# Taking the four 64x64 corners of TensorE diagonally in two attention products

## The chip, the cores and the metric

One core of a Trainium2 chip runs the kernel. The metric is device time in microseconds (us) of one execution; smaller is better. The median before is 263.3 us; executions of one kernel agree within 0.3%, and a change counts as faster or slower from 2% on. Shorter differences inside the kernel are read from the traces, which resolve single matmuls.

## The reference, cut to what matters

Inputs: q, k, v of 8 batches x 8 heads x 576 positions x 64, and two weight matrices, 512x2048 and 2048x512.

```python
q_s = exp(q - max(q, -1));  q_s = q_s / sum(q_s, -1)      # softmax over the 64 features
k_s = exp(k - max(k, 2));   k_s = k_s / sum(k_s, 2)       # softmax over the positions
kv  = einsum('bhsd,bhse->bhde', k_s, v)                   # the k-v product
x   = einsum('bhsd,bhde->bhse', q_s, kv)                  # x's product; heads side by side: 4608 x 512
h   = x @ w_in
out = (h * sigmoid(h)) @ w_out
```

## The kernel before

The two attention products have 64 rows and 64 columns of weights, a quarter of TensorE's 128x128 array. The kernel puts four of them into the array's four corners. A corner is a row half (the partitions that the operands come from) and a column half (the PSUM partitions of the output). In the k-v product `r` is the row half and `s` the column half; in x's product it is the other way round. Every corner writes a place of its own: another bank, or another half of the partitions.

```python
def kv(b, cc):                                   # 9 x 4 matmuls; kv_both is kv(b, 0), kv(b, 1)
    for j in range(J):                           # J = 9 groups of 64 positions, summed in PSUM
        for r in range(2):
            for s in range(2):
                nc.tensor.matmul(
                    out=PS[s * 64:(s + 1) * 64, 6 + r, cc * 128:cc * 128 + E1],          # E1 = 65
                    lhsT=ek[r * 64:(r + 1) * 64, j, (2 * cc + s) * D:(2 * cc + s + 1) * D],
                    rhs=vaug[r * 64:(r + 1) * 64, j, 2 * cc + s, :],
                    start=(j == 0), stop=(j == J - 1),
                )

def xt_mm(b, cc, col, n, bank, dst):             # one piece of n columns: 4 matmuls
    for r in range(2):
        for s in range(2):
            h = slice(s * 64, (s + 1) * 64)
            nc.tensor.matmul(
                out=PS[r * 64:(r + 1) * 64, bank + s, dst:dst + n],
                lhsT=kvn[b % 3][h, cc, r, :],
                rhs=st[b]["qT"][h, col // P:(col + n) // P, cc, r * 64:(r + 1) * 64],
            )

def xt(t, cc, eng=nc.scalar):                    # 512 columns: one or two pieces, then the copy out
    got = pieces(t)
    for b, col, n, dst in got:
        xt_mm(b, cc, col, n, 6, dst)
    xt_evac(t, cc, 6, got[0][3], TCH, got[0][3], eng)
# ... the feed-forward part: full-array matmuls of 256 columns in groups of eight (lines 368 and 468)
# ... a schedule that strews kv_both and xt between those groups, for the batch after next
```

The softmax here doesn't subtract the row's maximum and nothing guards it: scores larger than these inputs give would overflow.

Of the kernel before, what the change touches and what calls it, by code (L numbers as in the profile page):

```python
# [17 lines left out]
def kernel(  # L18
# [165 lines left out]

    def kv(b, cc):
        for j in range(J):
            for r in range(2):
                for s in range(2):
                    nc.tensor.matmul(  # L189
                        out=PS[s * 64:(s + 1) * 64, 6 + r, cc * 128:cc * 128 + E1],  # L190
                        lhsT=ek[r * 64:(r + 1) * 64, j, (2 * cc + s) * D:(2 * cc + s + 1) * D],
                        rhs=vaug[r * 64:(r + 1) * 64, j, 2 * cc + s, :],
                        start=(j == 0),
                        stop=(j == J - 1),
                    )
# [13 lines left out]
    def kv_both(b):  # L209
        kv(b, 0)  # L210
        kv(b, 1)
        kvcopy(b)
# [9 lines left out]
        return got  # L222

    def xt_mm(b, cc, col, n, bank, dst):
        for r in range(2):
            for s in range(2):
                h = slice(s * 64, (s + 1) * 64)
                nc.tensor.matmul(  # L228
                    out=PS[r * 64:(r + 1) * 64, bank + s, dst:dst + n],
                    lhsT=kvn[b % 3][h, cc, r, :],  # L230
                    rhs=st[b]["qT"][h, col // P:(col + n) // P, cc, r * 64:(r + 1) * 64],
                )
# [5 lines left out]
    def xt(t, cc, eng=nc.scalar):  # L238
# [4 lines that stand above are left out]
# [340 lines left out]
    trcopy(0, 0, 0, 5, 0, nc.scalar)  # L583
    trcopy(0, 0, 5, J, 1)
    kv(0, 0)
    kvcopy(0, 0, 1)
    tr(0, 1, 0, 5, 2)
    tr(0, 1, 5, J, 3)
    exp_k(0, 1)
    xt_mm(0, 0, 0, 320, 4, 0)  # L590
    xt_mm(0, 0, 320, 256, 0, 0)
    heat(3, 6)
    vcast(0, 1, nc.scalar, 0, 1)
# [257 lines left out]
```

## Time and profile before

| | before |
|---|---|
| median time | 263.3 us |
| TensorE busy | 252.6 us, 97% of the profiled span of 261.6 us |
| share of the end's chain: k-v (L189), x (L228) | 1.7%, 2.1% |
| one block of 72 k-v matmuls: first to last start | 0.592 us |
| one block of 8 x matmuls, two pieces of 256 columns: first to last start | 0.144 us |

"First to last start" of a block is taken from the records of the single matmuls in the trace. It is a better length than busy time here, since the records of some 17 matmuls (0.19 us each) overlap at any time in it. The records do not name the corner of a matmul. The lines behind the table are in the prediction.

### The profile page before, as it was taken

To read this page: it belongs to the slowest core of one execution; us is meant where nothing else is said; L and a number is where in the kernel's file an instruction comes from. 1 tells how busy PE (TensorE), PEld (TensorE's weight loads), DVE (VectorE), ACT (ScalarE), POOL (GpSimd) and SP (SyncE) were. 2 spreads that over 40 slices of the span, in tenths; PEclk is the share of its full clock that TensorE was granted. 3 is DMA by queue.
4 is the path that set the end of the run, shared out by engine and by line. 5 is a ranking of instruction groups with operands and counts; after the bars stand their busy time and mean duration, and the time that the engine had idled before them with its cause. 6 is when DMAs were issued, how large, how long until landed. Compare 5 with 4: busy or idle time off the path is not lost.

```text
span 261.6 us, 6410 instructions
## 1 busy us (share of the span) xinstructions
PE 252.6 (97%) x2732; PEld 203.2 (78%) x2732; DVE 207.7 (79%) x268; ACT 187.6 (72%) x212; POOL 65.7 (25%) x62
## 2 busy tenths in 40 slices
PE   8799999999999999999999999999999999999992
PEld 3457655656887888888888888888888888888881
DVE  2867797888997999799979997999798548855832
ACT  5766887898994799579957995799573748484610
POOL 1743791651160306030603060306000000000003
PEclk9999999999999999999999999999999999999999
DMA  7999999689979486957794869640534003300624
GB/s 244 335 192 297 299 319 333 259 184 391 307 278 238 111 220 230 205 142 189 262 230 118 218 233 167 180 89 3 90 76 87 3 0 78 85 3 1 139 64 120
DMA packets 35452, 45.89 MB, mean 175 GB/s; under 512 B 16208, under 2 KB 19984, under 8 KB 35424
## 3 DMA queue, kind: packets, MB, share of 16 engines
q1 hardware_dynamic: 29568, 33.69, 47.4%
q0 software_dynamic: 5616, 11.60, 17.0%
q8 instruction: 21, 0.34, 0.5%
q10 hardware_dynamic: 240, 0.20, 0.2%
q14 instruction: 7, 0.06, 0.1%
HBM read 36.70 MB, written 9.44 MB: 176 GB/s over the span
## 4 chain that ended last, share of the span: by engine, by line
PE 79%; DVE 6%; DMA 5%; issue 4%; POOL 3%; ACT 1%; POOLq 0%; DVEq 0%; ACTq 0%
PE PS L468 34%; PE PS L368 33%; PE PS L405 5%; DMA qt<-in_q_dram 5%; PE PS L276 2%; PE PS L228 2%; PE PS L189 2%; DVE h L346 1%; POOL W L545 1%; DVE S L442 1%; DVE GT L442 1%; DVE zq L148 1%; POOL out_dram L730 1%; POOL h L126 0%; DVE h L91 0%
## 5 line engine op out<-in xcount | busy, mean ns | idle before, releaser
L346 DVE TENSOR_TENSOR h<-PS,h 128x1024 f32<-128x1024 f32 (+1 forms) x45 | 54.0, 1199 | 13.0 <-ACT h L89 6.8
L468 PEld LDWEIGHTS <-GT 128*128 128x128 f16 x512 | 49.6, 98 | 6.8 <-issue 1.0
L368 PEld LDWEIGHTS <-WS 128*128 128x128 f16 x480 | 46.8, 98 | 7.2 <-issue 1.1
L468 PE MATMUL PS<-W,GT 128*128 128x256 f16 x384 | 49.1, 273 | 0.0
L368 PE MATMUL PS<-XS,WS 128*128 128x256 f16 (+1 forms) x360 | 46.3, 272 | 0.5 <-DVE h L346 0.5
L352 ACT ACTIVATE GT<-h 128x1024 f16<-128x1024 f32 (+1 forms) x45 | 46.1, 1047 | 0.3 <-DVE h L346 0.3
L89 ACT COPY h<-PS 128x1024 f32<-128x1024 f32 (+1 forms) x35 | 35.1, 1004 | 13.6 <-PE PS L368 13.1
L157 POOL TENSOR_TENSOR eq<-eq,rzq 128x1152 bf16<-128x1152 bf16 x13 | 27.8, 2135 | 58.2 <-DVE rzq L152 56.5
L468 PEld LDWEIGHTS <-S 128*128 128x128 f16 x384 | 37.1, 98 | 5.5 <-issue 1.0
L368 PEld LDWEIGHTS <-W 128*128 128x128 f16 x360 | 34.7, 98 | 4.8 <-issue 0.5
L468 PE MATMUL PS<-T,S 128*128 128x256 f16 x256 | 32.7, 273 | 0.0
L368 PE MATMUL PS<-XT,W 128*128 128x256 f16 (+1 forms) x240 | 29.5, 272 | 0.1
L352 ACT ACTIVATE GT<-PS 128x1024 f16<-128x1024 f32 (+1 forms) x15 | 15.3, 1017 | 18.9 <-PE PS L368 18.9
L91 POOL CAST vaug<-vt 128x1152 bf16<-128x1152 f32 x12 | 14.9, 1242 | 43.7 <-DMA vt<-in_v_dram 34.9
L108 ACT ACTIVATE eq<-qt 128x1152 bf16<-128x1152 f32 (+1 forms) x18 | 19.1, 1059 | 2.7 <-DMA qt<-in_q_dram 2.7
L730 POOL DMA_DIRECT2D out_dram<-ow x5 | 2.7, 546 | 72.5 <-DVE ow L715 72.5
L113 ACT ACTIVATE ek<-kt 128x1152 bf16<-128x1152 f32 x16 | 18.4, 1154 | 1.4 <-DMA kt<-in_k_dram 1.4
L148 DVE TENSOR_REDUCE zq<-eq 128x18 f32<-128x1152 bf16 x12 | 16.1, 1344 | 3.8 <-ACT eq L108 3.8
L258 PE MATMUL PS<-XT,W 128*128 128x288 f16 x128 | 16.6, 286 | 0.5 <-DVE XT L91 0.2
L468 PE MATMUL PS<-W,S 128*128 128x256 f16 x128 | 16.5, 273 | 0.0
L488 DVE SCALAR_TENSOR_TENSOR ow<-PS,sc 128x512 f32<-128x512 f32 x7 | 4.8, 691 | 14.4 <-ACT sc L484 14.4
L258 PEld LDWEIGHTS <-W 128*128 128x128 f16 x128 | 12.3, 97 | 4.9 <-issue 1.6
(78 smaller groups left out, 346.3 us busy)
## 6 DMA issues: line engine op xcount, KB each, us to landing
out_dram<-ow SPq DMA_DIRECT2D x64, 128.0 KB, 2.4
qt<-in_q_dram SPq DMA_DIRECT2D x12, 576.0 KB, 4.6
kt<-in_k_dram SPq DMA_DIRECT2D x12, 576.0 KB, 5.4
vt<-in_v_dram SPq DMA_DIRECT2D x12, 576.0 KB, 5.4
qt<-in_q_dram POOLq DMA_DIRECT2D x4, 576.0 KB, 10.6
kt<-in_k_dram POOLq DMA_DIRECT2D x4, 576.0 KB, 13.3
vt<-in_v_dram POOLq DMA_DIRECT2D x4, 576.0 KB, 12.7
W<-in_moe_w_out_dram POOLq DMA_DIRECT2D x4, 512.0 KB, 14.9
```

The lines of the kernel that those rows point to most:

```text
L89: eng.copy(out=o, in_=i)
L91: eng.tensor_copy(o, i)
L108: nc.scalar.activation(out=half(st[b]["eq"], cc)[:, :, g0:g1], in_=jgd(b, "qt", cc)[:, :, g0:g1], func=ACT.Exp)
L113: nc.scalar.activation(out=half(ek, cc), in_=jgd(b, "kt", cc), func=ACT.Exp)
L148: nc.vector.reduce_sum(out=z, in_=e, axis=AX.X)
L157: eng.tensor_tensor(out=e, in0=e, in1=r[:, :, :, None].to_broadcast([128, J, 2, D]), op=ALU.mult)
L258: nc.tensor.matmul(out=PS[:, 2 * (fb % 3) + n, 0:S // 2], lhsT=W1[:, c, fb * 128:(fb + 1) * 128], rhs=XTS[0][:, c, n * (S // 2):(n + 1) * ...
L346: nc.vector.tensor_tensor(out=four(t, i), in0=group_bank(t, True), in1=four(t, i), op=ALU.add)
L352: nc.scalar.activation(out=group_out(t, f, n), in_=x, func=ACT.Silu, scale=1.0 / XS)
L368: nc.tensor.matmul(out=PS[:, bank + p // 2, (p % 2) * HT:(p % 2) * HT + width(t)], lhsT=a[:, c, p * 128:(p + 1) * 128], rhs=bb[:, c, 0:wid ...
L405: nc.tensor.matmul(out=PS[:, 2 + tb, :], lhsT=GTS[t % 2][:, fc, tb * 128:(tb + 1) * 128], rhs=W2[:, fc, :], start=(fc == 0), stop=(fc == N ...
L468: nc.tensor.matmul(out=PS[:, bank, m * HN:(m + 1) * HN], lhsT=a[:, fc, m * 128:(m + 1) * 128], rhs=bb[:, fc, :], start=(first and fc == 0) ...
```

## The change

Its likely intent: neighbours in the program should not share a row half, so that a load of weights is never held up by a matmul that runs in the same rows. In each four, r = s comes first, then r != s. Only in the k-v product does the change follow it: its neighbours shared a row half before and no longer do. In x's product rows alternated before, and now the two middle matmuls of a four share one. Nothing else changes; line numbers after it move by one or two.

```diff
     def kv(b, cc):
         for j in range(J):
-            for r in range(2):
-                for s in range(2):
+            for i in range(2):
+                for r in range(2):
+                    s = r ^ i
                     nc.tensor.matmul(
...
     def xt_mm(b, cc, col, n, bank, dst):
-        for r in range(2):
-            for s in range(2):
+        for i in range(2):
+            for r in range(2):
+                s = r ^ i
                 h = slice(s * 64, (s + 1) * 64)
```

## The prediction

> **What bounds the kernel now.** I read the page first, then the chain of work that ended last, then the waits of TensorE, then the timeline of TensorE around the products that the change touches (line 189 is the k-v product, line 228 is x's product).
>
> The page, busy time by engine and the shares of the chain:
>
> ```profile
> PE 252.6 (97%) x2732; PEld 203.2 (78%) x2732; DVE 207.7 (79%) x268; ACT 187.6 (72%) x212; POOL 65.7 (25%) x62
> ...
> PE 79%; DVE 6%; DMA 5%; issue 4%; POOL 3%; ACT 1%; POOLq 0%; DVEq 0%; ACTq 0%
> PE PS L468 34%; PE PS L368 33%; PE PS L405 5%; DMA qt<-in_q_dram 5%; PE PS L276 2%; PE PS L228 2%; PE PS L189 2%; DVE h L346 1%; POOL W L545 1%; DVE S L442 1%; DVE GT L442 1%; DVE zq L148 1%; POOL out_dram L730 1%; POOL h L126 0%; DVE h L91 0%
> ```
>
> TensorE carries the end: 79% of the chain. Of that, the big feed-forward products (L468, L368) have two thirds of the span and the two changed lines some 2% each. The chain's own view prints them as 1.7% (L189) and 2.1% (L228) of 261.6 us, so 4.4 + 5.5 = 9.9 us. That is everything the change can reach, and most of it is arithmetic that stays.
>
> Waits of TensorE: every entry for a changed line. L228 does not appear at all.
>
> ```profile
> PE PS L189 <- ACT vaug L89: 0.3, 1, 0.3
> ```
>
> So these products are nearly never starved by another engine; what they cost is TensorE's own time. One steady stage of the chain (start, length, engine, line, count):
>
> ```profile
> 101.76 0.87 PE PS L368 x8
> 102.63 0.73 PE PS L189 x72
> 103.37 0.98 PE PS L368 x8
> ...
> 108.72 0.87 PE PS L368 x8
> 109.59 0.34 PE PS L228 x8
> 109.93 1.09 PE PS L468 x9
> ```
>
> A block of 72 k-v matmuls takes 0.73 us on the chain, and the group after it 0.98 instead of 0.87, so 0.84 us in all. A block of 8 x products takes 0.34, and the nine matmuls after it 1.09 where nine at 0.87/8 = 0.109 would take 0.98: 0.45 in all.
>
> Now the inside of the two blocks, from TensorE's timeline. The first answer below has a window that ends at 102.61, the second one at 102.64, the third covers the whole block; the fourth to sixth are an x block, cut at 109.64, at 109.70, and whole:
>
> ```profile
> 102.56 0.23 PE L189 MATMUL PS<-vaug,ek 64*64 64x65 bf16 x4
> ...
> 102.56 0.26 PE L189 MATMUL PS<-vaug,ek 64*64 64x65 bf16 x8
> ...
> 102.56 0.81 PE L189 MATMUL PS<-vaug,ek 64*64 64x65 bf16 x72
> ...
> 109.52 0.30 PE L228 MATMUL PS<-qT,kvn 64*64 64x256 bf16 x4
> ...
> 109.52 0.41 PE L228 MATMUL PS<-qT,kvn 64*64 64x256 bf16 x8
> ```
>
> Seventy-two matmuls of about 0.19 us each (the line's median is 193 ns) lie within 0.81 us, so some 17 are in flight at a time. They start in fours: four before 102.61, then four more. **All four corners already run together.** The x block says it too: four matmuls of 293 ns end 0.30 us after the first began, so their starts lie within 10 ns; the next four end 0.11 us later, and 0.11 us is what one stream of 256 columns takes in the full-array products (0.87/8 = 0.109). Four matmuls in a row would have taken 0.43.
>
> **What the Trainium skill says.** (1) "TensorE: Matmul & The Clock Gate", Part 3, The mechanism: matmuls in different tiles of the array run at the same time with starts about 4 ns apart, they start in program order, and a weight load overlaps matmuls in flight only when its row group differs. The first half agrees: the single records of the block at 102.56 show starts at 102.563, .567, .570 and .573. The second half is the obvious motive for the change, and the trace does not bear it out: k-v's order now is (row, column) (0,0), (0,1), (1,0), (1,1), so the second load has the row group of the matmul before it, yet its record starts at 102.565, 2 ns after that matmul, and is as long (103 ns) as the third, whose row group is new. (2) "TensorEngine Tiling (Array Packing)", Key Properties: changing the tiling mode drains TensorE. It agrees: the last full matmul before the block starts at 102.361, the first small one at 102.563, 0.20 us against the usual 0.109. The number of such switches does not change. (3) The first page again, "Wait — 56ns, not 53.3ns?": starts never come closer than about 25 ns however short the matmul. Not so here: 72 starts in 0.59 us are 8.3 ns apart.
>
> **The change, part by part.** It removes no instruction, adds none and moves no other engine's work: the same 576 k-v and 128 x pairs of weight load and matmul, permuted within each four. k-v goes to (0,0), (1,1), (0,1), (1,0): neighbours never share a row. x's product goes from (0,0), (1,0), (0,1), (1,1) to (0,0), (1,1), (1,0), (0,1): neighbours in a diagonal share nothing, but the middle pair now shares a row, where before rows alternated. Each output element has its own bank and partitions, and its sum over j keeps its order.
>
> *k-v.* The floor of the array: a full matmul of 256 columns takes 0.109 us, so 65 columns take about 0.0277 (estimate), and 18 fours take 0.50 us. Measured from first to last start: 0.592 us (102.563 to 103.155 in the records; the same 592 ns in six of the seven 72-blocks, 585 in the last). So at most 0.1 us a block could be won by any order. But the records say that the feed of instructions takes most of it: in the second half of the block the loads start evenly, 103.017, .025, .033, .042, .050, .058, .067: one pair of load and matmul every 8.33 ns. 71 x 8.33 = 591 ns, just the length of the block. In the first half the fours come every 32 ns on average (gaps of 36 and 29 by turns), hardly faster than 4 x 8.33 = 33.3. So the array waits for instructions by the middle of each block, and an order that lets it take a four in 29 instead of 32 ns only makes it catch up with the feed sooner. I allow 0 to 0.03 us a block: with 7 whole blocks and two halves in the prologue, 0 to 0.24 us.
>
> *x.* In the first four, the records show 134 ns to the second four: about 27 for the first weight load, which nothing can hide after the drain, and 107 for the stream. The second four's loads begin 27 ns into the block, under the first stream, and cost nothing. There is nothing in it to win: 0. If the shared row in the middle pair delayed that load, it would be by one load, 27 ns, in each of 16 first blocks: 0.4 us lost. I think it costs 0, since k-v has that very neighbourhood now and shows no delay.
>
> *Before and after.* Drains (0.09 us into the block, as much out of it) stay. The vector engine's wait for the last matmul moves by the few ns by which the last corner moves.
>
> Sum: between -0.24 and +0.4 us, most likely -0.05. Predicted 263.2 us.
>
> **Rivals.** *(A) The row-group rule holds and the loads are the bound.* Then k-v speeds up to the floor of 0.50 us: 0.09 x 8 = 0.7 us, 262.5 us. For it: an alternation of 36 and 29 ns that something in the array must cause. Against it: the even 8.33 ns of the second half. *(B) The diagonal pairs don't run four at once,* say because two column halves fed from different rows need something the straight pairs share. Then a k-v four takes two streams, 18 x 0.055 = 1.0 us in place of 0.59, +0.4 x 8 = 3.2 us, and each 512 columns of x take another 0.21 us, x 16 = 3.4 us: 270 us, +2.5%. Against it: all four are in flight at once already, (0,0) with (1,1) among them, so diagonals can share the array; only the order of issue is new. *(C) The reordering moves a wait.* Which matmul of a block carries the wait for a bank, and which ends it, changes; the block after may start some ns sooner or later, and the vector engine with it. TensorE waits 0.3 us for these lines in all, so at most +/-0.3 us.
>
> **Range and chances.** The three runs of the kernel before lie between 263.2 and 263.8, and that spread is larger than all effects I can derive. So the range is 262.7 to 263.8. Within 2% means 258.0 to 268.5. Faster than that would need over half of the 9.9 us on the path to vanish, below the array's floor: 1%. Slower needs rival B at full size: 2%. The rest, 97%, is "same".
>
> **What would show it.** In the changed profile: the 72-blocks of k-v still 0.81 us long, first to last start near 0.59 (0.50 would prove rival A, 1.0 rival B); x blocks still 0.41 long, with the second four 0.11 after the first; chain shares near 1.7% and 2.1%; same instruction count, 6410. The prediction is wrong if k-v's blocks get longer or shorter by over 0.05 us, or if a wait of TensorE by these lines appears that is not there now.

## The result, and the profile after

| | before | after |
|---|---|---|
| median of 4 runs each | 263.32 us (263.2 to 263.8) | 263.38 us (263.28 to 263.65) |
| ratio | | 1.000, 95% interval 0.998 to 1.002 |

The result is right, and the time is the same. (A ratio here is the mean time of one kernel's fast runs over that of the other's fast runs of the same rounds, so not quite the ratio of the medians quoted.)

The page of the changed kernel: busy times and the chain by line. The k-v product is now L190, x's product L230.

```profile
PE 251.8 (96%) x2732; PEld 203.1 (78%) x2732; DVE 208.0 (80%) x268; ACT 187.5 (72%) x212; POOL 65.6 (25%) x62
...
PE PS L470 34%; PE PS L370 33%; PE PS L407 5%; DMA vt<-in_v_dram 4%; PE PS L260 3%; PE PS L278 2%; PE PS L230 2%; PE PS L190 2%; DVE h L348 1%; DVE S L444 1%; DVE GT L444 1%; DVE zq L148 1%; SPq L97 1%; POOL out_dram L732 1%; ACT sg L252 1%
```

The chain still runs through the big products, and the two changed lines have their 2% each. The same stage of the chain as in the prediction (start, length, engine, line, count):

```profile
102.51 0.73 PE PS L190 x72
103.24 0.98 PE PS L370 x8
...
109.46 0.34 PE PS L230 x8
109.80 1.85 PE PS L470 x16
```

0.73 and 0.34 us, and 0.98 for the group after the k-v block: to the last digit the numbers of before. TensorE's timeline of the same blocks, with windows that end after the first four matmuls, after eight, and after all of them; then the first four and all eight of x:

```profile
102.44 0.22 PE L190 MATMUL PS<-vaug,ek 64*64 64x65 bf16 x4
...
102.44 0.26 PE L190 MATMUL PS<-vaug,ek 64*64 64x65 bf16 x8
...
102.44 0.81 PE L190 MATMUL PS<-vaug,ek 64*64 64x65 bf16 x72
...
109.39 0.30 PE L230 MATMUL PS<-qT,kvn 64*64 64x256 bf16 x4
...
109.39 0.41 PE L230 MATMUL PS<-qT,kvn 64*64 64x256 bf16 x8
```

Four at once, then four more, and the same 0.81 and 0.41 us. In the single records the first eight starts of this k-v block are at 0, 3 (before: 4), 7, 10, 53, 56, 59, 63 ns in both kernels, the fours after these follow each other every 29 to 39 ns in both, and a whole block measures 592 or 593 ns (585 and 586 in the last one).

One wait differs: TensorE's waits of the changed kernel have

```profile
PE PS L175 <- DVE eq L157: 1.5, 1, 1.5
...
PE PS L190 <- ACT vaug L89: 0.5, 2, 0.4
```

0.5 us in two waits where it was 0.3 in one, and 1.5 us for a transpose where it was 1.0. The longer wait for the transpose can't come from the change: TensorE's timeline shows that it ends before the first k-v matmul of the program has started. Before, then after:

```profile
8.65 0.68 PE L175 MATMUL PS<-ident,eq 128*128 128x128 bf16 x9 [0.96 <-DVE eq L157]
...
11.16 0.48 PE L189 MATMUL PS<-vaug,ek 64*64 64x65 bf16 x36 [0.33 <-ACT vaug L89]
```

```profile
8.67 0.68 PE L175 MATMUL PS<-ident,eq 128*128 128x128 bf16 x9 [1.52 <-DVE eq L157]
...
11.24 0.48 PE L190 MATMUL PS<-vaug,ek 64*64 64x65 bf16 x36 [0.39 <-ACT vaug L89]
```

The waits of the k-v product lie in the first 15 us too, where work hangs on the arrival of the inputs; x_runs2 below, with k-v's order of before, has two of 0.6 us together. A yardstick free of that is the distance from one k-v block to one three stages later, in the same trace. TensorE's timeline has, before,

```profile
102.56 0.81 PE L189 MATMUL PS<-vaug,ek 64*64 64x65 bf16 x72
...
181.14 0.78 PE L189 MATMUL PS<-vaug,ek 64*64 64x65 bf16 x72
```

and after

```profile
102.44 0.81 PE L190 MATMUL PS<-vaug,ek 64*64 64x65 bf16 x72
...
181.01 0.78 PE L190 MATMUL PS<-vaug,ek 64*64 64x65 bf16 x72
```

To the nanosecond the records give 78.575 us in both (102.563 to 181.138, 102.436 to 181.011). I call it the **three-stage distance** below; three k-v and six x blocks and all work between lie in it. So the change does nothing that these records show in the main loop. The question left is why the order is free: because any order is, or because this one is as good?

### The profile page after: what moved, and what is told of

Its sections match the earlier page's. It is cut to its first block, busy times and chain, and to the rows that moved or that the text cites. A ratio compares the mean times of both kernels' runs of the same rounds, so it can differ in the third digit from the quotient of the medians.

```text
span 261.5 us, 6410 instructions
## 1 busy us (share of the span) xinstructions
PE 251.8 (96%) x2732; PEld 203.1 (78%) x2732; DVE 208.0 (80%) x268; ACT 187.5 (72%) x212; POOL 65.6 (25%) x62
## 4 chain that ended last, share of the span: by engine, by line
PE 82%; DVE 7%; DMA 4%; ACT 2%; POOL 2%; issue 1%; SPq 1%; POOLq 0%; DVEq 0%; ACTq 0%
PE PS L470 34%; PE PS L370 33%; PE PS L407 5%; DMA vt<-in_v_dram 4%; PE PS L260 3%; PE PS L278 2%; PE PS L230 2%; PE PS L190 2%; DVE h L348 1%; DVE S L444 1%; DVE GT L444 1%; DVE zq L148 1%; SPq L97 1%; POOL out_dram L732 1%; ACT sg L252 1%
```

## The experiments

All start from the kernel before and alter only the order or the width of the changed products. Where one look was taken (no rounds), times are beside one run of the kernel before in the same call, the state of both is unknown (their granted clocks are 0.995 to 1.000), and they carry some tenths of a us of scatter (the kernel before alone: 263.12 to 263.76), so the block lengths and the three-stage distance decide.

### Each half of the change alone

`kv_only` has the diagonal order in the k-v product alone, `x_only` in x's product alone (the first and the second half of the diff above).

> The kernel before with k-v's order alone changed to the diagonal one, x's as before. Does the unchanged time hide two effects that cancel? Theory: no, blocks of 0.59 us, ratio 1.000 within the noise of +/-0.002. Rival G (k-v gains from alternating rows what x loses by the shared row in its middle pair): ratio 0.998 or less here and 1.002 or more in x_only.

> The kernel before with x's order alone changed. Theory: x blocks of two pieces of 256 columns stay at 0.144 us from first to last start, ratio 1.000 within +/-0.002. Rival G: ratio 1.002 or more, blocks 0.02 to 0.03 us longer.

Measured, five rounds: kv_only 263.12 us, ratio 0.9996 (0.9983 to 1.0010); x_only 263.24, ratio 1.0001 (0.9988 to 1.0013), before 263.21. Three-stage distances 78.574 and 78.576 us. The blocks of two pieces of 256 columns in x_only have 143 ns from first to last start, before 144. Nothing cancels; each half alone does nothing. Rival G is out.

### Two corners at a time, in the three possible pairs

Here the theory of the prediction (the feed of instructions limits a block, so the order is hidden) can be put to a harder test: with only two corners taking turns, the feed has time to spare, and a fault of the pair would show.

```diff
 kv_rows2:  for r in range(2):  for j in range(J):  for s in range(2):                 # a shared row half
 kv_cols2:  for s in range(2):  for j in range(J):  for r in range(2):                 # a shared column half
 kv_diag2:  for i in range(2):  for j in range(J):  for r in range(2):  s = r ^ i      # nothing shared
```

> From the kernel before: k-v's loop over r outermost, then j, then s, so that only two corners take turns, and the two share a row group: (0,0),(0,1),(0,0),(0,1)..., then the other row. Result stays right. Here the feed of 8.33 ns a pair of load and matmul (16.7 ns a step of two) is no longer the limit, the array is. Theory (order inside a step is free, corners only have to differ): a step of two takes 29 to 32 ns as a step of four does now, so 36 steps take 1.07 to 1.15 us from first to last start of a 72-block in place of 0.59, and the time is about 0.5 x 8 = 4 us longer, 267 us; the same as kv_cols2 and kv_diag2 within 0.03 us a block. Rival A (a load overlaps matmuls in flight only where its row group differs): every load waits for a stream of its row, a step takes about 54 ns, a block 1.95 us, 274 us, and kv_cols2 and kv_diag2 are far shorter.

> As kv_rows2, with s outermost: the two corners that take turns share a column half (one PSUM half, two banks) and differ in row group. Right result. Theory: 1.07 to 1.15 us a block, the same as kv_rows2, 267 us. Rival A: clearly shorter than kv_rows2, by up to 0.8 us a block.

> As kv_rows2, with the diagonal outermost: for i, for j, for r, s = r xor i, so the two corners that take turns share neither row nor column. Right result. Theory: 1.07 to 1.15 us a block, equal to the two others within 0.03, 267 us. Rival A: as kv_cols2, shorter than kv_rows2. If diagonal corners are the ones that can work together best (the motive of the change at its strongest), this one is the shortest of the three.

Measured: 265.09, 265.01 and 264.71 us beside 263.76; all right. TensorE's timeline of kv_rows2, then of kv_diag2:

```profile
103.27 1.04 PE L189 MATMUL PS<-vaug,ek 64*64 64x65 bf16 x72
```

```profile
102.86 1.04 PE L190 MATMUL PS<-vaug,ek 64*64 64x65 bf16 x72
```

The same length. From first to last start these blocks have 850, 849 and 851 ns, the three-stage distances are 79.288, 79.288 and 79.285 us. So a pair that shares a row half is neither slower nor faster than a diagonal one: rival A, that a load can't overlap a matmul of its own rows, is false here. (The 0.3 us by which kv_diag2's single time is shorter arise outside the three stages.)

But my number was wrong: I expected 1.07 to 1.15 us, 36 steps of 29 to 32 ns one after another, and a block took 0.85. The starts show how. A pair of one of these orders starts every 30 ns or so, but about 190 ns into a phase of 18 matmuls, when only 12 have started, two more starts follow after 6 to 9 ns, and for some 90 ns fours go by as in the full order. The next phase seems to have begun before the last one was done; kv_tags below tests that.

### One corner at a time, and with a tag on each

```diff
 kv_corner:  for r in range(2):  for s in range(2):  for j in range(J):
 kv_tags: the same, and
+                    n = E1 if j == 0 else E1 - 8 * r - 4 * s
-   out=PS[..., cc * 128:cc * 128 + E1]   rhs=vaug[..., :]
+   out=PS[..., cc * 128:cc * 128 + n]    rhs=vaug[..., 0:n]
```

> From the kernel before: k-v corner by corner, r and s outermost, j innermost, so that 9 matmuls in a row use one corner. Right result. It measures what the taking of turns is worth and whether a load can hide under a stream of its own corner. Theory: the loads hide (as they do in the full-array products), 72 steps of 29 to 32 ns, 2.1 to 2.3 us a block, +1.6 x 8 = 13 us, 276 us. Rival A: loads can't hide in their own row, 72 steps of 54 ns, 3.9 us a block, +26 us, 290 us.

> kv_corner again, but for j over 0 the four corners stream 65, 61, 57 and 53 columns (wrong result on purpose), so that the record of each matmul tells its corner. kv_rows2 and kv_corner came out shorter (0.85 and 1.58 us a block) than 36 and 72 steps one after another. Theory E (each corner has a short queue of its own, of about two pairs; the program is dealt out in order, but a corner starts its matmuls without regard to those of other corners that stand before them): matmuls of 61 columns start before the last two or three of 65 have, a few in each change of corner, block 1.55 to 1.6 us. Rival F (matmuls start strictly in program order; the shorter blocks come from faster steps in one corner): all of one width start before the first of the next.

kv_corner: 269.81 us beside 263.76, right. A block has 1.58 us from first to last start, less than both numbers expected. Its timeline:

```profile
105.06 1.77 PE L189 MATMUL PS<-vaug,ek 64*64 64x65 bf16 x72
```

In the main loop the time follows the blocks: 0.99 us longer each, three-stage distance 81.479 against 78.575, so +0.97 a stage. (The whole kernel is only 6.05 us longer in these single times, not 8 x 0.99 = 7.9: of the four blocks' worth, 4.0 us, before the main loop, 2.5 us show in the start of its first k-v block.)

kv_tags has blocks of 1.58 us again (269.47 us). Its output is wrong, which doesn't matter for the time. Now every record but those of the first j has its corner in its width: 9 matmuls of the first corner, all of 65 columns, come first in the program; then the second corner's first of 65 and eight of 61. Groups by shape in a window from the block's start (104.70) to 104.945; it holds all of the block's matmuls that had started by then:

```profile
L190 PE MATMUL PS<-vaug,ek 64*64 64x65 bf16 x8 | 0.4, 197 | 0.0
L369 PE MATMUL PS<-XT,W 128*128 128x256 f16 x1 | 0.3, 272 | 0.0
L190 PE MATMUL PS<-vaug,ek 64*64 64x61 bf16 x1 | 0.2, 193 | 0.0
```

A 61 has started when only eight 65s have, though ten 65s stand before it in the program. The starts from the records, in ns from the block's first: 65 at 0, 52, 88, 117, 150, 179, 185, 215; **61 at 237**; 65 at 244; 61 at 271; 65 at 276. So matmuls of different corners overtake each other. Theory E is borne out and rival F is not: at 237 two of the first corner's still wait (taking each corner by itself in program order). (The 65 at 185, 6 ns after another one where a corner takes some 30, must be the second corner's first; then three were waiting. None goes ahead of more in this block.)

### How far the overtaking reaches

If each corner has its own short queue, then the order of the program is free as long as no corner has more in a row than its queue holds. `kv_runs3` gives each corner three j in a row; `x_runs2` gives each corner both pieces of x in a row.

```diff
 kv_runs3:
-        for j in range(J):
+        for j0 in range(0, J, 3):
             for r in range(2):
                 for s in range(2):
+                    for j in range(j0, j0 + 3):
 x_runs2 (in xt):
-        for b, col, n, dst in got:
-            xt_mm(b, cc, col, n, 6, dst)
+        for r in range(2):
+            for s in range(2):
+                for b, col, n, dst in got:
+                    one matmul as in xt_mm
```

> k-v in runs of three: j in three groups of 3, and in each group corner by corner, three j in a row. Right result. Theory E: two waiting pairs of a corner don't stop the next corner, so a run of 3 (one at work, two waiting) costs nearly nothing: a 72-block of 0.60 to 0.65 us, time 263.3 to 264. Rival F: the third matmul of a run starts 62 ns after its first and those of the next corner after that, so 24 runs of about 62 ns and more, a block of 1.4 to 1.5 us, time 270.

> x's product from the main loop corner by corner: each corner takes both its pieces in a row (a run of two; the prologue's calls stay as they are). Right result. Theory E: a second piece waits in its corner's own queue while the next corner starts: a block of two pieces of 256 columns stays at about 0.15 us from first to last start and 0.41 in all, time 263.3. Rival F: the next corner's first piece can't start before this corner's second, 134 ns for the first corner and 107 for each other, about 0.45 us from first to last start, +0.3 us in each of 12 blocks of two pieces, 267 us.

kv_runs3: 263.89 us beside 263.35, right. Its timeline, and that of x_runs2's x block of two pieces:

```profile
102.69 0.90 PE L190 MATMUL PS<-vaug,ek 64*64 64x65 bf16 x72
```

```profile
109.74 0.42 PE L239 MATMUL PS<-qT,kvn 64*64 64x256 bf16 x8
```

First to last start is 0.708 us in kv_runs3 (0.682 in the last block): more than the 0.60 to 0.65 that I gave theory E, and half of the 1.4 to 1.5 of rival F. A run of three isn't quite free; it costs 0.095 us a stage (three-stage distance 78.860). The first four starts are at 0, 10, 20 and 30 ns. They must be the beginnings of the four corners, three places of the program apart, so the fourth corner begins 30 ns after the first instead of 10; and near the middle of the block two steps of four starts take 48 and 62 ns. x_runs2: 263.73 us beside 263.35, the block 0.154 us from first to last start in place of 0.144, where rival F asked for 0.45. The 10 ns are the later begin of the fourth corner (starts at 109.740, .746, .753, .760). Three-stage distance 78.640, +0.022 a stage for two x blocks. So a run of two costs next to nothing, and the permutation within a four, which gives no corner two in a row, nothing.

### What does limit a block

Two limits were candidates: the array (stream and load of weights) and the feed of instructions. `kv_short` streams half as many columns; `kv_wide` and `kv_wide_diag` stream 128, so that the array is the limit beyond doubt, in the straight and in the diagonal order.

```diff
 kv_short:      n = 65 if j == 0 else 33;  out=PS[..., cc * 128:cc * 128 + n],  rhs=vaug[..., 0:n]
 kv_wide:       out=PS[..., cc * 128:cc * 128 + 128],  rhs = the first 128 of the 130 columns of heads 2cc, 2cc + 1
 kv_wide_diag:  as kv_wide, with the changed kernel's loops
```

> From the kernel before, its order kept: for j over 0 the k-v matmuls stream 33 of the 65 columns (wrong result on purpose: the columns from 33 on keep the first j's sum). Same number of instructions. Theory (the feed of one pair of load and matmul every 8.33 ns is the limit): a 72-block stays at 0.59 us from first to last start, with loads evenly 8.3 ns apart sooner than before, time 263.3. Rival C (the stream in the array is the limit): a four takes half as long, a block 0.30 to 0.35 us, time 2 us shorter. Rival D (the loading of 64 weight columns, about 27 ns, is the limit of a corner): a block 0.50 to 0.52 us.

> From the kernel before, its order kept: every k-v matmul streams 128 columns (those of both heads of its pair) in place of 65 (wrong result on purpose for s = 1). Now the array and not the feed is the limit while all four corners are at work. Theory: a four takes 128 columns at 0.109 us per 256 = 55 ns, a block 17 x 55 + 27 + 10 = 0.97 us from first to last start; time +0.38 x 8 = 3 us, 266.3 us; kv_wide_diag is the same within 0.03 us a block. Rival A: the loads that share a row come late, a block is 1.2 us or more.

> As kv_wide with k-v's order of the changed kernel (diagonal fours). Theory: 0.97 us a block as kv_wide, within 0.03; so the change does nothing where the array is the limit either. Rival A, and the motive of the change: shorter than kv_wide by 0.1 us a block or more, and the time by 1 us or more.

All three are wrong on purpose. kv_short took 263.22 us beside 263.12; its timeline:

```profile
102.41 0.79 PE L190 MATMUL PS<-vaug,ek 64*64 64x65 bf16 x72
```

(0.79 and not 0.81, since the last record itself is shorter.) A block has 591 or 592 ns from first to last start as before (584 in the last), with half the stream. So the stream is not the limit, and this run's rival C is out. In its first half the fours come evenly every 31 to 32 ns (before: about 29 and 36 by turns), though streaming 33 columns takes only 14 ns (half of the 0.0277 us estimated for 65): something in a corner other than the stream takes 31 to 32 ns a matmul. That part of rival D holds; the weight load is its likely cause, but no run separates it from a fixed minimum of a corner.

In the second half the loads come one every 8.3 ns (at 405, 413, 421, 430, 438, 446 ns), as before; I had expected this even pace to begin sooner, and it doesn't. The stream doesn't set it, then. That it is the feed of instructions is my inference; no run changes the feed. And it doesn't set a block's length by itself, as the prediction's 71 x 8.33 = 591 ns has it. In the kernel before, the 68th load starts at 530 ns, 28 ahead of that sum's line (67 x 8.33 = 558), and then, in every 72-block but the last, there is a gap of 34 ns before the last four loads, whose cause the records don't show. The last block has no such gap; its last load starts at 563 ns and its last matmul still at 585. There the corners set the end. So two limits lie 5% apart, the 32 ns that a corner takes for its matmul in each four and the 33.3 ns of four loads at the even pace, and these runs don't say more exactly how they share a block.

kv_wide and kv_wide_diag took 265.64 and 265.24 us. TensorE's timeline of the one, then of the other:

```profile
103.19 1.20 PE L189 MATMUL PS<-vaug,ek 64*64 64x128 bf16 x72
```

```profile
102.80 1.20 PE L190 MATMUL PS<-vaug,ek 64*64 64x128 bf16 x72
```

989 ns from first to last start in both (0.97 expected), and a three-stage distance of 79.770 us in both. Fours come every 56 ns, the stream of 128 columns. Where the array is the limit and the feed has time to spare, the diagonal order is still worth nothing, as with two corners above. The feed, then, is not what hides the order. What fits all runs is that the corners work independently: a load waits for its own corner, whatever its neighbour in the program does, as far as the short queues reach.

## Why the prediction was right

The time (263.2 predicted, 263.38 measured) and the class were right. By its steps:

- **All four corners already run together; the x block has nothing to win.** Shown: 0.30 and 0.41 us in both kernels, and x_only alone is at ratio 1.0001. The fear of 27 ns for the shared row in x's middle pair was empty, as I thought.
- **A load may overlap a matmul of its own row half.** Right, and now shown where nothing could hide it: kv_rows2 and kv_diag2 have the same blocks.
- **The feed takes what an order could win, 0 to 0.03 us a block.** The number was right (0 to 1 ns in every whole block), but in part by luck. The even 8.33 ns is there, yet 71 x 8.33 meets the block's length to the nanosecond only because of the gap before its last four loads. I also supposed that another order might let the array take a four in 29 instead of 32 ns, and that the feed would then hide it. There is nothing to hide: the first fours are the same, and with the feed out of the way, in kv_rows2 and kv_diag2 and in both wide runs, the orders are still equal.
- **What I missed** is the overtaking. I thought of starts in program order, and so took the trace's neighbours for the program's, which the records can't tell. That is why I expected 1.07 us and more for two corners at a time and got 0.85. As kv_tags and kv_runs3 have it, permuting a four changes only the order in which four independent queues are handed one pair each.
- **Rival B** (diagonal pairs can't run at once, 270 us) was false; the prediction's **rival C** (a wait moves) did not show: the wait that grew most, by 0.5 us, ends before the first changed matmul, and the k-v product's 0.2 us more have their like in x_runs2, with the old order.

## What to carry to other kernels

Where the trace shows the corners of the array already starting together, expect little from permuting matmuls that stand next to each other (here it was worth nothing); count instead how many in a row go to one corner: here runs of two cost 10 ns in a block of 8, and runs of three and nine 0.1 and 1.0 us in a block of 72. Check a sum that meets the measured length against the records between its ends: 71 x 8.33 ns met it by luck. Compare short blocks by their starts and by the distance between the same instruction in two stages of one trace: it told 10 ns here, where the time as a whole scatters by hundreds. And test a mechanism that explains "no effect" where it should give an effect: the two-corner runs gave the right verdict and a wrong number, and the wrong number led to the cause.

## What the Trainium skill lacked or had wrong

- "TensorE: Matmul & The Clock Gate", Part 3, The mechanism: it says that matmuls start and end strictly in program order. In kv_tags, matmuls of the second corner start at 237 and 271 ns while two of the first corner, which stand before them, start at 244 and 276. The page's advice that the last matmul alone may signal the end should be read with that in mind; in kv_tags, the only run that tells corners apart, a block's last matmul in the program also started last.
- The same place: a weight load overlaps matmuls in flight only when the row group differs (the text above that list makes an exception for the background weight buffer). Two corners that share rows take 850 ns a block, two that don't 851.
- The same page, "Wait — 56ns, not 53.3ns?": starts are never closer than about 25 ns. It doesn't say that this can't hold across tiles, for which Part 3 has 4 ns. Over four corners starts are 8.3 ns apart on average here, 3 ns within a four. In one corner, with a load for each matmul, the spacing was 31 to 32 ns for 33 columns (kv_short) and for 65 (kv_corner).
- "TensorEngine Tiling (Array Packing)" says that tiles work independently, but no page has the depth for one tile: in kv_tags the next corner got ahead of two to three waiting pairs and no more, and 72 matmuls in runs of 1, 3 and 9 took 0.592, 0.708 and 1.58 us.
- No page has a pace like that of the loads in the second half of a block, 8.33 ns for a pair of load and matmul. That it is the rate of the instructions is argued, not shown.
